# Rank of the score matmuls in a hand-made instruction order, and a scaling that two engines may take

## The chip, the cores and the metric

The kernel runs on one core of one Trainium2 chip. A core has five engines with a queue of instructions each: TensorE (PE, with its weight loads shown as PEld), VectorE (DVE), ScalarE (ACT), GpSimd (POOL) and SyncE (SP), which here issues most DMAs. Every engine works through its own queue in order and waits on semaphores for the others. The time is the device time of one execution in microseconds (us); where several runs are shown, their median.

## The reference, cut to what matters

Block-sparse attention (4 batches, 8 heads, 768 positions, 64 columns per head; blocks of 32) is followed by four causal attention "experts" on its output, of which each position uses the best two, weighted.

```python
mask = np.abs(blk_i - blk_j) <= 1
mask = mask | (blk_i == 0) | (blk_j == 0) | (blk_i == n_blocks - 1) | (blk_j == n_blocks - 1)
# and three sampled blocks of keys for every block of queries
attn = softmax(where(mask, scale * q @ k.T, -1e9));  x = attn @ v      # heads side by side: 512 columns
logits = x @ w_gate;  topk = best 2 of 4;  w = softmax over the two
for e in range(4):
    a = softmax(causal(scale * (x @ wq[e]) @ (x @ wk[e]).T))           # 768 x 768
    out += (w of e, 0 where not chosen) * (a @ (x @ wv[e]) @ wo[e])
```

## The kernel before, in words

**Units of work.** For each batch the sparse part works through six tiles of 128 queries, each in two halves of four heads: `tiles` (lines 645 to 724), called a U unit. Its scores (L671) put, for each block of 32 queries, the three neighbouring, three sampled and two end blocks of keys in a score tile `s`; one reduction on DVE (L676) takes the maxima, four exponents on ACT (L681) write the probabilities into a tile `p`, four transposes on PE in each of two steps (L687) and their copies (L383 on ACT or L387 on DVE) put them into `pt`, PV (L701) multiplies by the gathered values `va` and `vb`, DVE divides by the sums (L711 to L713), and two transposes (L718) with a split into a high and a low half (L399, L400) write x into `xh` and `xl`. The first and the last block of queries see all keys: `ends` (lines 576 to 643), two G units per batch, with scores L590 in two chunks of 512 and 256 keys, reductions L596, exponents L599, transposes L607, PV L616 and L626 to L635. They read their own scaled copy of the queries, `qz`.

The expert part projects x: `project_v` (L744), `project_qk` (L801, three products of high and low halves), and `gating`. `expert` (lines 808 to 891) handles one row of 128 positions of a pair of experts: scores L822 with the triangle added at L826, reductions L832, exponents L835 with their sums, a few small DVE operations for the denominators (L846 to L852), the scaling of the probabilities by 1/sum and gate weight (L859, on DVE), transposes L870, PV L887 and a split (L399, L400). Rows 4 and 5 have more than 512 keys: two score chunks, two `p` tiles, two `pt` tiles and four scalings; the other rows have one of each and two scalings. `project_o` (L901) multiplies by wo and stores.

**Loads.** Keys, queries and values come by DMA from SP. From batch 1 on the queries are scaled on POOL (L443, for `q` and `qz`), sampled keys are copied together on POOL (L501), values get a column of ones on POOL (L469), go to a scratch tensor in DRAM (L479) and are gathered from there for each tile of queries: neighbours and end blocks at L545 to L557 into `va` and `vb`, sampled blocks at L564, twelve DMAs for a tile.

**What sets the order.** Nothing is scheduled by a compiler. The program lists all units in a sequence (lines 932 to 939), where the projections of a batch are merged with the last sparse tiles of it and the first of the next batch, and the experts of a batch with the G units and the tiles 2 and 3 of the next. `Plan` (lines 66 to 193) then plays the list through with a cost for each operation: whenever an engine is free, it takes of the operations whose inputs are done the one with the lowest rank, `prio`, and issues it there and then. The rank of an operation is the place n of its unit in the sequence, (n, 0), unless it is given; ties go by the order in which operations were added. What `Plan` chooses is the fixed order in each engine's queue. An operation with several engines is offered to each of them, in the order ACT, DVE, PE, POOL, SP, and goes to the first that takes it. An operation is held back while its unit is more than `window` places ahead of the oldest unfinished unit, a DMA while its rank is more than `look` places ahead; and while the buffers it needs are all taken.

**Buffers.** Tiles come from rings (lines 231 to 257): two score tiles `s` and four tiles `w` in PSUM; four `p`, three `pt`, two `xn`, four `q`, two tiles of gathered keys, and one `va` and one `vb` for even and one for odd tiles of queries. A ring's slot is taken by the first operation that writes it and comes free with the last that reads it. A score operation takes its `s` tile and its `p` tiles at once; `pt` is taken by the first transpose and held until PV.

The functions that the change touches:

Of the kernel before, what the change touches and what calls it, by code (L numbers as in the profile page):

```python
# [14 lines left out]
ALU = mybir.AluOpType  # L15
# [3 lines left out]
SP = mybir.EngineType.SP  # L19
ACT = mybir.EngineType.Activation  # L20
DVE = mybir.EngineType.DVE
POOL = mybir.EngineType.Pool
# [174 lines left out]
def block_sparse_then_moe(ctx: ExitStack, tc: tile.TileContext, qT, kT, v, samp, wg, wq, wk, wv, wo, out):  # L197
    nc = tc.nc
# [10 lines left out]
    scale = 1.0 / float(D) ** 0.5  # L209
# [11 lines left out]
    def f(ap):  # L221
        return ap.bitcast(F32)

    pl = Plan(window=10, look=12, lat={"PE": 0.2, "ACT": 0.12, "DVE": 0.12, "POOL": 0.15, "SP": 0.1})

    def ring(name, n, shape, dt=F32, space=None, ordered=False):
        p = space or pool
# [210 lines left out]
    def scaled(b, n, q):  # L438

        if b == 0:  # L440
            copy(n, lambda: q.t, lambda: q.t, [(q, "raw")], [q], mul=scale)
        else:
            pl.add("POOL", 0.25 + 0.0012 * n, lambda: nc.gpsimd.tensor_scalar(q.t, q.t, scale, None, op0=ALU.mult),  # L443
                   r=[(q, "raw")], w=[q])

    def load_ends(b):
# [12 lines left out]
    def load_values(b):  # L459

        vn, d = rVN.get(), rScr.get()
        for t0 in range(0, NT, 2):
            ts = slice(t0, t0 + 2)
            if b:
                for t in (t0, t0 + 1):
                    x = rW.get()
                    dma(b, 0.5, lambda e, x=x, t=t: e.dma_start(x.t, v[b, 128 * t:128 * t + 128].rearrange("p h c -> p (h c)")),
                        w=[x], xfer=0.7)
                    pl.add("POOL", 0.9, lambda x=x, t=t: nc.gpsimd.tensor_copy(  # L469
                        vn.t[:, t, :, 0:D], x.t.rearrange("p (h c) -> p h c", h=H)), r=[x, "c_1"], w=[vn, (vn, t0)])  # L470
            else:
                x = rPT.get()
                y = lambda x=x: x.t.rearrange("p (t c) d -> p t (c d)", t=2)
                dma(b, 0.5, lambda e, y=y, t0=t0: e.dma_start(
                    y(), v[b, 128 * t0:128 * t0 + 256].rearrange("(t p) h c -> p t (h c)", p=128)), w=[x], xfer=1.4)
                for t in (t0, t0 + 1):
                    copy(512, lambda t=t: vn.t[:, t, :, 0:D], lambda y=y, i=t - t0: y()[:, i].rearrange("p (h c) -> p h c", h=H),
                         [x, "c_1"], [vn, (vn, t0)])
            dma(b, 0.6, lambda e, t0=t0, ts=ts: e.dma_start(  # L479
                d.t[128 * t0:128 * t0 + 256].rearrange("(t p) h c -> p t (h c)", p=128),  # L480
                vn.t[:, ts].rearrange("p t h c -> p t (h c)")), both=False, r=[(vn, t0), "zr"], w=[d], xfer=1.9)
        return vn, d
# [93 lines left out]
    def ends(b, pp_, st, X, unit):  # L576


        qz, k, vn = st["qz"], st["k"], st["vn"]
        ss, pps, pts = ([r.get() for _ in range(2)] for r in (rs, rP, rPT))  # L580
        sm, xb, o = rSm.get(), rW.get(), rw.get()
        pairs = (2 * pp_, 2 * pp_ + 1)
        chunks = ((0, 512), (512, 256))

        def sc(i, c0, cw):
            for j in range(2):
                for c, P4 in enumerate(pairs):
                    r = slice(64 * j, 64 * j + 64)
                    x = k.t + P4 * S + c0
                    nc.tensor.matmul(ss[i].t[64 * c:64 * c + 64, j, 0:cw], qz.t[r, P4], KK[r, x:x + cw],  # L590
                                     start=True, stop=True, tile_position=(64 * j, 64 * c), skip_group_check=True)

        for i, (c0, cw) in enumerate(chunks):
            pl.add("PE", 0.96 if cw == 512 else 0.5, lambda i=i, c0=c0, cw=cw: sc(i, c0, cw),
                   r=[qz] + [(k, P4) for P4 in pairs], w=[ss[i]] + [(x, "r") for x in pps], unit=unit)
            pl.add("DVE", 0.15 + 0.00208 * cw, lambda i=i, cw=cw: nc.vector.tensor_reduce(  # L596
                sm.t[:, 2 * i:2 * i + 2], ss[i].t[:, :, 0:cw], AX.X, op=ALU.max, negate=True), r=[ss[i]], w=[(sm, "m", i)], unit=unit)
            for j in range(2):
                pl.add("ACT", 0.27 + 0.00083 * cw, lambda i=i, j=j, c0=c0, cw=cw: nc.scalar.activation(  # L599
                    pps[j].t[:, c0:c0 + cw], ss[i].t[:, j, 0:cw], AF.Exp, bias=sm.t[:, 2 * i + j:2 * i + j + 1]),  # L600
                    r=[ss[i], (sm, "m", i)], w=[(pps[j], i)], unit=unit)
        chunk_factors(sm, unit)
        for j in range(2):
            for c0, n in ((0, 4), (4, 2)):
                w = rw.get()
                pl.add("PE", 0.09 + 0.11 * n, lambda j=j, c0=c0, n=n, w=w: [
                    nc.tensor.transpose(w.t[:, 128 * i:128 * i + 128], pps[j].t[:, 128 * (c0 + i):128 * (c0 + i) + 128], ident)  # L607
                    for i in range(n)], r=[(pps[j], 0 if c0 == 0 else 1), "c_a"], w=[w, (pts[j], "r")], unit=unit)
                evacuate(128 * n, lambda j=j, c0=c0, n=n: pts[j].t[:, c0:c0 + n].rearrange("p a b -> p (a b)"),
                         lambda w=w, n=n: w.t[:, 0:128 * n], [w], [pts[j]], unit=unit)  # L610

        def pv(j):
            for t in range(NT):
                x = (2 * (t // 4) + j) * VW
                for c, P4 in enumerate(pairs):
                    nc.tensor.matmul(o.t[64 * c:64 * c + 64, x:x + VW], pts[j].t[:, t, 64 * c:64 * c + 64],  # L616
                                     vn.t[:, t, 2 * P4 + j], start=t % 4 == 0, stop=t in (3, NT - 1), tile_position=(0, 64 * c),
                                     skip_group_check=True)

        for j in range(2):  # L620
            pl.add("PE", 0.85, lambda j=j: pv(j), r=pts + [vn], w=[o, (xb, "r")], unit=unit)

        def norm():
            ov = o.t[:, 0:4 * VW].rearrange("p (n c) -> p n c", c=VW)
            y = xb.t[:, 0:4 * VW].rearrange("p (n c) -> p n c", c=VW)
            nc.vector.tensor_tensor(y, ov, sm.t[:, 10:14, None].to_broadcast([128, 4, VW]), op=ALU.mult)  # L626
            nc.vector.tensor_tensor(y[:, 0:2], y[:, 0:2], y[:, 2:4], op=ALU.add)
            nc.vector.tensor_scalar(sm.t[:, 4:6], y[:, 0:2, D], EPS, None, op0=ALU.add)
            nc.vector.reciprocal(sm.t[:, 4:6], sm.t[:, 4:6])
            nc.vector.tensor_tensor(xb.t[:, 384:512].rearrange("p (j d) -> p j d", j=2), y[:, 0:2, 0:D],  # L630
                                    sm.t[:, 4:6, None].to_broadcast([128, 2, D]), op=ALU.mult)

        pl.add("DVE", 1.3, norm, r=[o, (sm, "e")], w=[xb, (sm, "n")], unit=unit)
        w = rw.get()
        pl.add("PE", 0.2, lambda: nc.tensor.transpose(w.t[:, 0:128], xb.t[:, 384:512], ident), r=[xb],  # L635
               w=[w, (X[0], "r"), (X[1], "r")], unit=unit)

        def at(x):
            x = x[:, pairs[0]]
            return sub_ap(x, 0, [x.ap[0], [S, 2], [S - 32, 2], [1, 32]])  # L640

        split(128, lambda: at(XH), lambda: at(XL), lambda: w.t[:, 0:128].rearrange("p (c a b) -> p c a b", c=2, a=2),
              [w], [(x, P4, "g") for x in X for P4 in pairs], unit)

    def tiles(b, t, pp_, st, X, unit):
# [3 lines left out]
        pairs = (2 * pp_, 2 * pp_ + 1)  # L649
# [22 lines left out]
                                         tile_position=(64 * j, 32 * g), skip_group_check=True)  # L672

        for i in range(2):
            pl.add("PE", 0.62, lambda i=i: sc(i), r=[q, (k, pairs[i]), kg], w=[s, (pp, "r")], unit=unit)
        pl.add("DVE", 1.22, lambda: nc.vector.tensor_reduce(sm.t[:, 0:4], s.t.rearrange("p j (t c) -> p (j t) c", t=2),  # L676
                                                            AX.X, op=ALU.max, negate=True), r=[s], w=[(sm, "m")], unit=unit)
        for i in range(2):
# [129 lines left out]
    def expert(b, st, p, r, unit):  # L808
# [19 lines left out]
        for i, (c0, cw) in enumerate(chunks):  # L828
            rd = [(qk, 0, 512 if r > 3 else 0), (qk, 1, 512 if c0 else 0), "c_b"]
            pl.add("PE", 0.08 + cw / 520 + (0.2 if c0 + cw == n else 0.0), lambda i=i, c0=c0, cw=cw: sc(i, c0, cw),  # L830
                   r=rd, w=[ss[i]] + [(x, "r") for x in pps], unit=unit)
            pl.add("DVE", 0.15 + 0.00208 * cw, lambda i=i, cw=cw: nc.vector.tensor_reduce(  # L832
                sm.t[:, 2 * i:2 * i + 2], ss[i].t[:, :, 0:cw], AX.X, op=ALU.max, negate=True), r=[ss[i]], w=[(sm, "m", i)], unit=unit)
            for j in range(2):
# [20 lines left out]
        for i, (c0, cw) in enumerate(chunks):  # L855
            for j in range(2):
                x = 10 + 2 * i + j
                f_ = lambda j=j, c0=c0, cw=cw: pps[j].t[:, p0[j] + c0:p0[j] + c0 + cw]
                pl.add("DVE", 0.13 + 0.00052 * cw, lambda f_=f_, x=x: nc.vector.tensor_scalar(  # L859
                    f_(), f_(), sm.t[:, x:x + 1], None, op0=ALU.mult),  # L860
                    r=[(pps[j], j, i), (sm, "d")], w=[(pps[j], j, "n", i)], unit=unit)
        pts = [rPT.get() for _ in range(2)] if two else [rPT.get()] * 2
        t0s = (0, 0) if two else (0, 4)
# [150 lines left out]
```

## Time and profile before

| | |
|---|---|
| median of 3 runs | 598.55 us (597.52 to 602.64) |
| the profiled execution | 603.58 us |
| its span, first to last instruction | 601.8 us |
| mean granted clock of PE | 0.963 |

The profile is that of one execution, and all numbers of stages and instructions below come from it. A busy share is the share of the span in which an engine had an instruction under way. A row of a group reads: line, engine, operation, what it writes <- what it reads, shapes, count | busy time in us, mean of one in ns | idle time of that engine just before, and what ended it. A row of waits reads: who waited <- for what: us in total, times, the longest. "PE w L607 <- ACT p L599" means that PE stood before the instruction of line 607 that writes `w`, until ACT's instruction of line 599 that writes `p` had ended. In a timeline row, start and duration in us stand in front and the idle time before it in brackets. The granted clock is TensorE's, as a share of full speed; it is either 1.00 or 0.50 at any moment, and a stretch's value is the mean.

| 40 equal slices of the span | |
|---|---|
| PE busy, tenths | 2787889967799999989799999998799999997896 |
| PE clock, tenths | 9899989978799999999799999999799999999999 |
| POOL busy, tenths | 2867604610002033413001211532101202000000 |

### The profile page before, as it was taken

How to read it: one execution, taken by the hardware profiler on the slowest of the kernel's cores; microseconds unless marked ns; L12 is line 12 of the kernel's file. 1: busy time of each engine (PE TensorE's matmuls, PEld its weight loads, DVE VectorE, ACT ScalarE, POOL GpSimd, SP SyncE). 2: the span in 40 equal slices, each digit the busy share in tenths (PEclk: the TensorE clock that was granted, in tenths of full speed). 3: DMA queues.
4: the chain of work that ended last, by engine and by line, in shares of the span. 5: the costliest groups of instructions: out<-in, count | busy, mean ns of one | idle time of the engine just before them, and what ended most of it. 6: DMA issues, size and time to landing. Idle time of an engine off the chain costs nothing.

```text
span 601.8 us, 23159 instructions
## 1 busy us (share of the span) xinstructions
PE 533.3 (89%) x9416; PEld 405.5 (67%) x9416; DVE 380.0 (63%) x1028; ACT 305.2 (51%) x844; POOL 138.8 (23%) x334
## 2 busy tenths in 40 slices
PE   2787889967799999989799999998799999997896
PEld 1576677854377688867556778886457678776674
DVE  4788644636687744446687873464787885356794
ACT  2576453535556654345474654353566564334654
POOL 2867604610002033413001211532101202000000
PEclk9899989978799999999799999999799999999999
DMA  7544467776110467775401274876601153000011
GB/s 254 175 105 122 95 173 244 207 184 168 43 38 20 119 196 221 209 173 137 108 2 53 62 205 117 290 169 169 153 2 36 37 145 103 21 2 1 2 36 71
DMA packets 58410, 70.25 MB, mean 117 GB/s; under 512 B 17792, under 2 KB 30208, under 8 KB 58304
## 3 DMA queue, kind: packets, MB, share of 16 engines
q1 hardware_dynamic: 53440, 65.88, 40.0%
q10 hardware_dynamic: 4864, 2.89, 1.6%
q8 instruction: 75, 1.23, 0.9%
q14 instruction: 31, 0.25, 0.2%
HBM read 55.92 MB, written 12.81 MB: 114 GB/s over the span
## 4 chain that ended last, share of the span: by engine, by line
PE 71%; DVE 14%; ACT 4%; issue 4%; DMA 2%; SPq 1%; POOL 0%; POOLq 0%; ACTq 0%; DVEq 0%
PE w L801 11%; PE s L671 9%; PE s L822 7%; PE w L701 7%; PE w L687 7%; PE w L887 7%; PE w L901 6%; PE w L744 5%; PE w L870 5%; DVE p L859 2%; DVE sm L832 2%; PE w L718 2%; ACT pt L383 2%; PE w L607 2%; PE w L616 1%
## 5 line engine op out<-in xcount | busy, mean ns | idle before, releaser
L383 ACT ACTIVATE pt<-w 128x512 f32<-128x512 f32 (+3 forms) x149 | 77.7, 543 | 70.6 <-PE w L870 28.8
L681 ACT ACTIVATE p<-s,sm 128x256 f32<-128x256 f32 x192 | 77.2, 478 | 46.2 <-DVE sm L676 46.0
L501 POOL COPY KK<-KK 128x128 f32 x213 | 54.2, 302 | 137.8 <-PE s L671 85.6
L835 ACT ACTIVATE p<-s,sm 128x512 f32<-128x512 f32 (+3 forms) x128 | 68.5, 545 | 18.5 <-DVE sm L832 13.8
L676 DVE TENSOR_REDUCE sm<-s 128x4 f32<-128x1024 f32 x48 | 58.5, 1221 | 27.1 <-PE s L671 26.8
L387 DVE COPY pt<-w 128x512 f32<-128x512 f32 (+3 forms) x91 | 52.6, 587 | 34.9 <-PE w L687 26.8
L443 POOL TENSOR_SCALAR q<-q 128x512 f32<-128x512 f32 x18 | 27.2, 1514 | 187.7 <-DMA q<-in_qT_dram 187.7
L832 DVE TENSOR_REDUCE sm<-s 128x2 f32<-128x1024 f32 (+3 forms) x64 | 54.3, 854 | 25.1 <-PE s L826 15.4
L671 PE MATMUL s<-KK,q 64*32 64x64 f32 (+1 forms) x3072 | 64.2, 278 | 3.8 <-ACT q L383 1.3
L671 PEld LDWEIGHTS s<-KK,q 64*32 64x32 f32 x3072 | 51.4, 107 | 17.3 <-issue 9.3
L687 PE MATMUL w<-ident,p 128*128 128x128 f32 x384 | 58.0, 282 | 2.9 <-ACT p L681 2.9
L822 PE MATMUL s<-qk 64*128 64x512 f32 (+3 forms) x256 | 58.8, 541 | 0.4 <-ACT p L681 0.3
L870 PE MATMUL w<-ident,p 128*128 128x128 f32 x336 | 50.5, 284 | 7.0 <-DVE p L859 5.4
L701 PE MATMUL w<-vb,pt 128*32 128x65 f32 x1536 | 50.5, 221 | 5.6 <-issue 5.6
L887 PE MATMUL w<-pt,vb 128*64 128x128 f32 x672 | 51.3, 282 | 3.4 <-DVE pt L387 1.9
L701 PE MATMUL w<-va,pt 128*32 128x65 f32 x1536 | 50.8, 224 | 3.5 <-issue 2.5
L887 PEld LDWEIGHTS w<-pt,vb 128*64 128x64 f32 x672 | 38.0, 138 | 19.9 <-DVE pt L387 5.3
L687 PEld LDWEIGHTS w<-ident,p 128*128 128x128 f32 x384 | 43.3, 143 | 10.4 <-ACT p L681 4.1
L870 PEld LDWEIGHTS w<-ident,p 128*128 128x128 f32 x336 | 37.5, 143 | 14.1 <-DVE p L859 3.4
L859 DVE TENSOR_SCALAR p<-p,sm 128x512 f32<-128x512 f32 (+3 forms) x128 | 46.0, 405 | 1.2
L701 PEld LDWEIGHTS w<-va,pt 128*32 128x32 f32 x1536 | 36.2, 109 | 15.2 <-issue 7.1
L801 PE MATMUL w<-xh,wqkh 128*128 128x512 f32 (+1 forms) x128 | 46.0, 359 | 0.0
(122 smaller groups left out, 951.0 us busy)
## 6 DMA issues: line engine op xcount, KB each, us to landing
vb<-scr SPq DMA_DIRECT2D x270, 65.0 KB, 2.7
va<-scr SPq DMA_DIRECT2D x12, 780.0 KB, 6.3
scr<-VN SPq DMA_DIRECT2D x12, 520.0 KB, 3.6
KK<-in_kT_dram SPq DMA_DIRECT2D x16, 384.0 KB, 5.6
out_dram<-ws SPq DMA_DIRECT2D x24, 256.0 KB, 2.2
ws<-in_v_dram SPq DMA_DIRECT2D x18, 256.0 KB, 4.1
q<-in_qT_dram SPq DMA_DIRECT2D x18, 256.0 KB, 4.2
va<-scr SPq DMA_DIRECT2D x6, 585.0 KB, 5.6
```

The costliest lines, as they stand in the source:

```text
L383: nc.scalar.activation(dst(), src(), AF.Copy, scale=1.0 if mul is None else mul)
L671: nc.tensor.matmul(dst, q.t[r, P4, 32 * g:32 * g + 32], src, start=True, stop=True, tile_position=(64 * j, 32 * g), skip_group_check=True)
L676: pl.add("DVE", 1.22, lambda: nc.vector.tensor_reduce(sm.t[:, 0:4], s.t.rearrange("p j (t c) -> p (j t) c", t=2), AX.X, op=ALU.max, negate ...
L681: pl.add("ACT", 0.47, lambda i=i, j=j, n=n: nc.scalar.activation(pp.t[:, 256 * n:256 * n + 256], s.t[:, j, 256 * i:256 * i + 256], AF.Exp, ...
L687: nc.tensor.transpose(w.t[:, 128 * c:128 * c + 128], pp.t[:, 512 * (c // 2) + 256 * i + 128 * (c % 2):][:, 0:128], ident)
L701: nc.tensor.matmul(o.t[32 * g:32 * g + 32, VW * n:VW * n + VW], pt.t[:, 4 * i + 2 * j + c, 32 * g:32 * g + 32], x.t[:, cl(g), h * VW:h * V ...
L801: nc.tensor.matmul(w.t[:, 0:cw], a[:, k, x], y[:, k, c0:c0 + cw], start=n == 0, stop=n == 3 * KT - 1)
L822: nc.tensor.matmul(ss[i].t[:, j, 0:cw], qk.t[x, 0, r * 128:(r + 1) * 128], qk.t[x, 1, c0:c0 + cw], start=True, stop=not last, tile_positio ...
L832: pl.add("DVE", 0.15 + 0.00208 * cw, lambda i=i, cw=cw: nc.vector.tensor_reduce(sm.t[:, 2 * i:2 * i + 2], ss[i].t[:, :, 0:cw], AX.X, op=AL ...
L835: pl.add("ACT", 0.47 + 0.00083 * cw, lambda i=i, j=j, c0=c0, cw=cw: nc.scalar.activation(pps[j].t[:, p0[j] + c0:p0[j] + c0 + cw], ss[i].t[ ...
L870: nc.tensor.transpose(w.t[:, 128 * i:128 * i + 128], pps[j].t[:, p0[j] + 128 * t:][:, 0:128], ident)
L887: nc.tensor.matmul(o.t[64 * j:64 * j + 64, 0:128], vb.t[:, t, e * D:(e + 1) * D], pts[j].t[:, t0s[j] + t], start=t == 0, stop=t == r, tile ...
```

## The change

- The score operations of the three kinds of units (L590, L671, L822 with L826) get the rank of the place six before their unit's, `(unit - AHEAD, 0)`. All else of a unit keeps its rank.
- `window` goes from 10 to 14, `look` from 12 to 16.
- The scaling of queries on POOL (L443) becomes a multiplication by the scale and a second one by 1.0 in one instruction.
- The scaling of experts' probabilities (L859) is offered to DVE and POOL; POOL's form multiplies by the factor of each row and by 1.0.
- `Plan`'s costs change for the scaling of queries (0.25 + 0.0012 n to 0.15 + 0.00095 n us), the copy of values on POOL (0.9 to 0.63) and DVE's scaling of probabilities (0.00052 to 0.00056 per column).

```diff
--- before.py
+++ after.py
@@ -221,7 +221,8 @@
     def f(ap):
         return ap.bitcast(F32)
 
-    pl = Plan(window=10, look=12, lat={"PE": 0.2, "ACT": 0.12, "DVE": 0.12, "POOL": 0.15, "SP": 0.1})
+    AHEAD = 6
+    pl = Plan(window=14, look=16, lat={"PE": 0.2, "ACT": 0.12, "DVE": 0.12, "POOL": 0.15, "SP": 0.1})
 
     def ring(name, n, shape, dt=F32, space=None, ordered=False):
         p = space or pool
@@ -440,7 +441,7 @@
         if b == 0:
             copy(n, lambda: q.t, lambda: q.t, [(q, "raw")], [q], mul=scale)
         else:
-            pl.add("POOL", 0.25 + 0.0012 * n, lambda: nc.gpsimd.tensor_scalar(q.t, q.t, scale, None, op0=ALU.mult),
+            pl.add("POOL", 0.15 + 0.00095 * n, lambda: nc.gpsimd.tensor_scalar(q.t, q.t, scale, 1.0, op0=ALU.mult, op1=ALU.mult),
                    r=[(q, "raw")], w=[q])
 
     def load_ends(b):
@@ -466,7 +467,7 @@
                     x = rW.get()
                     dma(b, 0.5, lambda e, x=x, t=t: e.dma_start(x.t, v[b, 128 * t:128 * t + 128].rearrange("p h c -> p (h c)")),
                         w=[x], xfer=0.7)
-                    pl.add("POOL", 0.9, lambda x=x, t=t: nc.gpsimd.tensor_copy(
+                    pl.add("POOL", 0.63, lambda x=x, t=t: nc.gpsimd.tensor_copy(
                         vn.t[:, t, :, 0:D], x.t.rearrange("p (h c) -> p h c", h=H)), r=[x, "c_1"], w=[vn, (vn, t0)])
             else:
                 x = rPT.get()
@@ -592,7 +593,8 @@
 
         for i, (c0, cw) in enumerate(chunks):
             pl.add("PE", 0.96 if cw == 512 else 0.5, lambda i=i, c0=c0, cw=cw: sc(i, c0, cw),
-                   r=[qz] + [(k, P4) for P4 in pairs], w=[ss[i]] + [(x, "r") for x in pps], unit=unit)
+                   r=[qz] + [(k, P4) for P4 in pairs], w=[ss[i]] + [(x, "r") for x in pps], unit=unit,
+                   prio=(unit - AHEAD, 0))
             pl.add("DVE", 0.15 + 0.00208 * cw, lambda i=i, cw=cw: nc.vector.tensor_reduce(
                 sm.t[:, 2 * i:2 * i + 2], ss[i].t[:, :, 0:cw], AX.X, op=ALU.max, negate=True), r=[ss[i]], w=[(sm, "m", i)], unit=unit)
             for j in range(2):
@@ -672,7 +674,7 @@
                                          tile_position=(64 * j, 32 * g), skip_group_check=True)
 
         for i in range(2):
-            pl.add("PE", 0.62, lambda i=i: sc(i), r=[q, (k, pairs[i]), kg], w=[s, (pp, "r")], unit=unit)
+            pl.add("PE", 0.62, lambda i=i: sc(i), r=[q, (k, pairs[i]), kg], w=[s, (pp, "r")], unit=unit, prio=(unit - AHEAD, 0))
         pl.add("DVE", 1.22, lambda: nc.vector.tensor_reduce(sm.t[:, 0:4], s.t.rearrange("p j (t c) -> p (j t) c", t=2),
                                                             AX.X, op=ALU.max, negate=True), r=[s], w=[(sm, "m")], unit=unit)
         for i in range(2):
@@ -828,7 +830,8 @@
         for i, (c0, cw) in enumerate(chunks):
             rd = [(qk, 0, 512 if r > 3 else 0), (qk, 1, 512 if c0 else 0), "c_b"]
             pl.add("PE", 0.08 + cw / 520 + (0.2 if c0 + cw == n else 0.0), lambda i=i, c0=c0, cw=cw: sc(i, c0, cw),
-                   r=rd, w=[ss[i]] + [(x, "r") for x in pps], unit=unit)
+                   r=rd, w=[ss[i]] + [(x, "r") for x in pps], unit=unit,
+                   prio=(unit - AHEAD, 0))
             pl.add("DVE", 0.15 + 0.00208 * cw, lambda i=i, cw=cw: nc.vector.tensor_reduce(
                 sm.t[:, 2 * i:2 * i + 2], ss[i].t[:, :, 0:cw], AX.X, op=ALU.max, negate=True), r=[ss[i]], w=[(sm, "m", i)], unit=unit)
             for j in range(2):
@@ -856,8 +859,9 @@
             for j in range(2):
                 x = 10 + 2 * i + j
                 f_ = lambda j=j, c0=c0, cw=cw: pps[j].t[:, p0[j] + c0:p0[j] + c0 + cw]
-                pl.add("DVE", 0.13 + 0.00052 * cw, lambda f_=f_, x=x: nc.vector.tensor_scalar(
-                    f_(), f_(), sm.t[:, x:x + 1], None, op0=ALU.mult),
+                pl.add(("DVE", "POOL"), (0.13 + 0.00056 * cw, 0.15 + 0.00095 * cw), (
+                    lambda f_=f_, x=x: nc.vector.tensor_scalar(f_(), f_(), sm.t[:, x:x + 1], None, op0=ALU.mult),
+                    lambda f_=f_, x=x: nc.gpsimd.tensor_scalar(f_(), f_(), sm.t[:, x:x + 1], 1.0, op0=ALU.mult, op1=ALU.mult)),
                     r=[(pps[j], j, i), (sm, "d")], w=[(pps[j], j, "n", i)], unit=unit)
         pts = [rPT.get() for _ in range(2)] if two else [rPT.get()] * 2
         t0s = (0, 0) if two else (0, 4)
```

## The prediction

> **What bounds the kernel now.** I read the page first (engine totals), then the stretches by stage with the granted clock, then the waits inside those stages.
>
> ```profile
> span 601.8 us, 23159 instructions
> PE 533.3 (89%) x9416; PEld 405.5 (67%) x9416; DVE 380.0 (63%) x1028; ACT 305.2 (51%) x844; POOL 138.8 (23%) x334
> ```
>
> TensorE (PE) sets the time; nothing in this change takes a matmul away. A gain can only come from PE's idle time, 601.8 - 533.3 = 68.5 us, and from time in which PE runs at half clock. So I looked for both by stage. The rows of the stage view give PE, PEld, DVE, ACT and POOL busy time, then the granted clock, the DMA share and GB/s.
>
> ```profile
> 136.00:160.00 24.00, 17.59 (x285) 10.95 (x281) 17.37 (x54) 13.39 (x37) 1.49 (x1) 0.91 0.52 127
> 281.00:306.30 25.30, 20.93 (x250) 12.87 (x250) 18.98 (x56) 13.98 (x42) 2.80 (x7) 0.87 0.33 78
> 425.50:446.50 21.00, 16.23 (x160) 10.18 (x156) 15.18 (x45) 10.66 (x30) 1.62 (x1) 0.84 0.38 92
> 48.00:77.00 29.00, 21.64 (x594) 17.22 (x582) 20.26 (x48) 16.35 (x42) 18.83 (x33) 1.00 0.47 110
> 549.00:568.20 19.20, 14.18 (x121) 9.73 (x119) 14.27 (x46) 12.07 (x40) 0.00 (x0) 0.91 0.01 1
> ```
>
> The first three are the heads of the expert phases of batches 0, 1 and 2: PE idles 24.0 - 17.59 = 6.4, 4.4 and 4.8 us, together 15.6. The fourth is the stage with the weights (7.4 idle), the fifth the head of the last batch's experts (5.0). The clock by stretch shows where it is halved:
>
> ```profile
> 145.60:149.00 3.40, 3.40 (x17) 1.63 (x17) 1.78 (x3) 1.19 (x4) 1.30 (x1) 0.50 0.96 263
> 159.30:166.10 6.80, 5.86 (x18) 2.01 (x20) 2.38 (x6) 2.77 (x8) 0.00 (x0) 0.50 0.00 0
> 289.00:295.80 6.80, 5.33 (x46) 3.17 (x48) 2.88 (x7) 2.26 (x7) 0.00 (x0) 0.50 0.61 147
> 428.90:435.80 6.90, 4.91 (x38) 2.75 (x40) 3.40 (x7) 1.84 (x5) 0.69 (x1) 0.51 0.70 160
> 77.40:80.80 3.40, 3.40 (x23) 3.17 (x30) 0.96 (x2) 1.76 (x4) 0.00 (x0) 0.50 0.37 81
> 555.20:558.60 3.40, 3.02 (x14) 2.69 (x16) 2.76 (x9) 1.64 (x5) 0.00 (x0) 0.50 0.00 0
> 128.60:135.40 6.80, 5.26 (x39) 3.55 (x38) 2.52 (x6) 1.05 (x3) 0.00 (x0) 0.50 0.59 154
> 268.50:271.90 3.40, 3.40 (x16) 3.16 (x16) 1.12 (x4) 0.56 (x2) 0.43 (x1) 0.50 0.74 196
> ```
>
> Each lies in or just behind a stage with stalls. PE work at half clock costs about half its duration: in the four stretches of the expert heads (3.40 + 5.86 + 5.33 + 4.91) / 2 = 9.75 us. What PE waited for, one view for each of the stages (expert heads in order, weights, last batch):
>
> ```profile
> PE w L607 <- ACT p L599: 2.2, 1, 2.2
> PE s L590 <- ACT p L835: 1.5, 2, 1.2
> ...
> PE w L607 <- ACT p L599: 3.0, 2, 2.6
> ...
> PE w L607 <- ACT p L599: 3.7, 2, 3.3
> ...
> PE w L718 <- DVE xn L713: 3.0, 2, 1.8
> PE w L687 <- ACT p L681: 2.9, 3, 1.9
> ...
> PE w L870 <- DVE p L859: 4.1, 3, 2.3
> ```
>
> At the expert heads PE mostly waits at the transposes of an "ends" unit (L607), because its scores (L590) were issued just before and reduction, exponent and transposes follow one another. Its inputs had been there long: for batch 1 the scaled qz is ready at 218.6 us, and the wait at L607 ends at 290.47.
>
> ```profile
> 217.79 0.85 POOL L443 TENSOR_SCALAR qz<-qz 128x256 f32<-128x256 f32 x1 [0.25 <-DMA qz<-in_qT_dram]
> 290.47 0.69 PE L607 MATMUL w<-ident,p 128*128 128x128 f32 x2 [2.62 <-ACT p L599]
> ```
>
> **The change part by part.**
>
> *Scores six places ahead (expert heads).* No instruction is added; scores at L590, L671 and L822 take a lower rank, so PE issues them as soon as a score tile (ring s, 2) and a probability tile (ring p, 4) are free, during the projections at L801, which is work for PE alone. Reductions and exponents then run under cover, and the projections held back fill what was idle. Of the 15.6 us, 2.2 + 1.5 + 3.0 + 3.7 = 10.4 (two thirds) end at an ends unit, which can be brought forward; the rest hangs on experts whose q and k come from the projection itself. Reachable: 15.6 + 9.75 = 25.3 us. Bounds 0 and -25.3; I take 60%, a little under the two thirds since two score tiles limit the lead: **-15.2**.
>
> *Weights stage.* Reachable 7.4 + 3.40 / 2 = 9.1. DVE and POOL are at 20.26 and 18.83 of 29 there, so scores alone feed engines that are already loaded. Bounds 0 and -9.1; I take a third: **-3.0**.
>
> *Last batch.* Reachable 5.0 + 3.02 / 2 = 6.5. No other unit covers the experts here, and most of it ends with the scaling at L859, which the next unit's early scores can cover in part. Bounds 0 and -6.5; about half: **-3.0**.
>
> *POOL shares L859.* Prices: DVE's rows (last batch) and POOL's for 128x512, and what happened where both ran at once.
>
> ```profile
> L859 DVE TENSOR_SCALAR p<-p,sm 128x512 f32<-128x512 f32 x12 | 5.3, 483 | 0.2
> L859 DVE TENSOR_SCALAR p<-p,sm 128x256 f32<-128x256 f32 x8 | 2.4, 348 | 0.0
> L469 POOL COPY VN<-ws 128x512 f32<-128x512 f32 x18 | 10.8, 618 | 2.0 <-DMA ws<-in_v_dram 1.8
> L443 POOL TENSOR_SCALAR q<-q 128x512 f32<-128x512 f32 x18 | 27.2, 1514 | 187.7 <-DMA q<-in_qT_dram 187.7
> 427.98 1.62 POOL L443 TENSOR_SCALAR q<-q 128x512 f32<-128x512 f32 x1 [5.89 <-DMA q<-in_qT_dram]
> 428.04 1.70 DVE L859 TENSOR_SCALAR p<-p,sm 128x512 f32<-128x512 f32 x3
> ```
>
> The three DVE scalings beside POOL's instruction took 1.70 us instead of 0.48 + 0.35 + 0.35 = 1.18: such pairs get in each other's way. The two-multiplication form has no row. Bounds: 0.62 (a copy of that size) and 2 x 1.51 = 3.03 (two passes of today's form). The new plan says 0.64 for it; where its other new figures have a row (the copy of v 0.63 against 0.618, DVE's scaling 0.42 against 0.483) they fit within 15%, so I go by the low end, though the nearest row by operation is 1.51. A two-chunk expert has four scalings, now 2 x 0.48 + 2 x 0.35 = 1.66 us in a row. If POOL takes one of each size at 0.62 and about 0.45 and the engines overlap fully, 1.07; if they take turns, 0.48 + 0.62 + 0.35 + 0.45 = 1.90. At 1.51 and about 0.85 in turns: 3.19. In three batches PE has other units, so the price is nothing while that cover lasts; without it, each unit would add its difference to PE's wait. In the last batch (4 two-chunk units, 8 others with half as much work, so 8 in effect) it is 8 x -0.6 = -5, 8 x +0.24 = +2 or 8 x +1.5 = +12. I take turns in part: **+1.0**.
> The Trainium skill, "SBUF — State Buffer", section "Who interferes with whom", says that DVE in a two-port mode and GpSimd share a port pair that one holds for its whole instruction; the 1.70 against 1.18 agrees. By that rule the term is +2 and not +1, the result 585.0.
>
> *Loads and gathers.* A score issues no DMA, but frees its q and gathered-key tiles earlier, so POOL's copies (L501) and q's loads start earlier, loads also by look 12 to 16, on the same SP queue as the gathers of v. Gathers already end four stalls of PE (the views of 100 to 135, 255 to 270 and 400 to 412 us; "issue" here is a wait for a landing that the view doesn't name):
>
> ```profile
> PE w L701 <- issue: 5.0, 2, 4.7
> PE s L671 <- POOL q L443: 1.1, 1, 1.1
> PE s L671 <- POOL KK L501: 0.2, 1, 0.2
> ...
> PE w L801 <- issue: 1.8, 1, 1.8
> PE s L671 <- issue: 0.9, 1, 0.9
> ...
> PE w L701 <- issue: 2.3, 1, 2.3
> ...
> 271.69 8.80 SPq L564 DMA_DIRECT2D vb<-scr  x12
> vb<-scr SPq DMA_DIRECT2D x270, 65.0 KB, 2.7
> ```
>
> That is 10.0 us, and (5.26 + 3.40) / 2 = 4.3 at half clock. One tile's gather is 8.80 us of issue and 2.7 to landing, and it starts when the tile two before has left va/vb through PV, which earlier scores push back. PE also gets there sooner. Bounds -10 (stalls gone) and +12 (one gather, 11.5, once more); I take **+3.0**.
>
> *q scaled on POOL in the other form; new costs.* 18 instructions at 0.62 to 3.03 instead of 1.51. POOL is busy 23%, and PE waited for this line once (1.1 us, the row above), so the work of other tiles hides it; bounds -1, and +5 where a longer one blocks DVE as at 428 us. I take **0**. The lower planned costs of copying v change only order.
>
> *Older work behind a score.* PE works in order: if a score's input is late on the chip, the older transposes and PV behind it wait, and ACT and DVE for their results. Scores' waits on POOL came to 1.3 us before (q 1.1, KK 0.2). Bounds 0 and +10; I take **+2.6**, twice those.
>
> Sum: -15.2 - 3.0 - 3.0 + 1.0 + 0 + 3.0 + 2.6 = -14.6. The profiled execution took 603.6 us (span 601.8, 1.8 around it), which makes 589.0; it lies 5.0 above the median of the runs, 598.55, so I forecast **584.0** (-2.4%).
> The Trainium skill, "TensorE: Matmul & The Clock Gate", Part 1, has the clock halved after an idle window of about 3.4 us. Here it is 0.50 at 289.0 though the longest stall of that stage is 2.6, so the trace decides; by the page the 9.75 would not go with these stalls, and the result would be 0.6 x 9.75 = 5.9 later, 589.9.
>
> **The rivals.**
> 1. *All chain stalls go:* -25.3 - 9.1 - 6.5 + 3.0 = -37.9, so 560.6. For it: inputs lie ready 70 us. Against: two score tiles, and expert heads need the projection.
> 2. *Gathers take the gain:* PE arrives about 6 us earlier per batch at a gather that SP issues no sooner, three times: -21.2 + 18 = -3, 595.5. For it: the 4.7 us wait. Against: PE hides gathers elsewhere (only 10 us of waits in all).
> 3. *Slower: tiles take the three pt slots.* Younger tiles, now through their exponent early, get transposed in a gap and hold pt until PV, which needs their gather of v (11.5 us); an expert or ends unit needs two slots and stands still. Three stages at 11.5, half covered, are +17; with half of the 15.2 kept, +9.5: 608. It decides from the second such stage on. For it: pt has 3 slots and L701 already waits for gathers. Against: older transposes still rank first.
> 4. *POOL's form stays at 1.51:* +12 in place of +1: 595.
> 5. *The lead does not come about:* rings s and p are full, a quarter of 21.2 remains and the give-back of 3.0: -2.3, 596.
>
> **How the numbers follow.** Forecast 0.47 (its own range 574 to 592), rivals in order 0.12, 0.13, 0.16, 0.05, 0.07. A measurement of this kernel can tell about 1% (592.6 and 604.5) from no change. Faster: forecast and rival 1, 0.59, and a little of the others, 0.60; same: rivals 2, 4 and 5, 0.24; slower: rival 3, 0.16. The range 562 to 608 leaves out about half of rival 1 and half of rival 3, near 0.14.
>
> **What would show it.** Right: no wait at L607 for L599 over 1 us in the expert heads; PE idle there under 8 us in sum; clock 0.95 or more in those stages; POOL's new scalings of 128x512 near 0.64 us; about half of L859's instructions on POOL, and DVE's 128x512 ones above 483 ns where POOL runs beside them. Wrong: waits L701 <- issue that grow past 10 us (rival 2), waits of L870 or L607 behind tiles' PV (rival 3), POOL's form at 1.5 us or more (rival 4), or L590 again within 5 us of its L607 (rival 5).

## The result and the profile after

The changed kernel takes 565.6 us (median of 4 runs, 564.6 to 569.6) against 600.6 us for the kernel before beside it: a ratio of 0.943, 95% interval 0.936 to 0.951, so 5.7% faster. The forecast was 584.0 us, 2.4% faster; the measured time is 18 us below it, outside the forecast's own range of 574 to 592 and near the rival that had all chain stalls go (560.6). Runs more than 1.5% above the fastest of their kernel (three of b_window's ten, one of the kernel before) are left out of the medians and ratios below.

The page after, its span and its totals of the engines:

```profile
span 564.8 us, 23268 instructions
PE 511.7 (91%) x9416; PEld 398.2 (71%) x9416; DVE 373.4 (66%) x972; ACT 286.6 (51%) x813; POOL 173.1 (31%) x421
```

Of the 37.0 us between the two spans, PE's idle time gave 68.5 - 53.1 = 15.4 and its busy time 21.6. PE work at half clock fell from 38.0 to 13.4 us (all half-clock stretches of the two profiles, the short ones at the start included), at half its duration 12.3; the other 9.3 us of busy time I can't put down to one cause. The profiled execution of before was 5 us above the 598.55 us of the first table and had more half-clock time than the same kernel in a hardly different order (b_jit below: 21.1 us of PE work), so part of the 12.3 belongs to that execution.

Where the expert phases begin (from the last projection of q and k of a batch to its first output projection), first the three stages of before, then those of after; columns as in the stage view of the prediction:

```profile
121.30:173.60 52.30, 40.84 (x621) 25.91 (x619) 31.20 (x87) 24.63 (x66) 4.47 (x13) 0.84 0.47 113
276.30:314.00 37.70, 33.19 (x455) 20.84 (x453) 28.70 (x75) 21.82 (x60) 4.46 (x13) 0.91 0.27 65
416.00:454.30 38.30, 33.25 (x457) 20.90 (x454) 29.41 (x75) 21.91 (x60) 5.78 (x14) 0.91 0.32 78
```

```profile
123.10:161.60 38.50, 33.55 (x573) 23.08 (x572) 29.43 (x77) 20.41 (x63) 7.15 (x11) 1.00 0.65 153
262.90:290.50 27.60, 25.64 (x344) 17.10 (x342) 23.66 (x63) 18.11 (x52) 6.62 (x11) 1.00 0.32 79
397.70:425.30 27.60, 25.65 (x344) 17.10 (x343) 24.04 (x63) 18.09 (x52) 6.62 (x11) 1.00 0.32 77
```

PE's idle time there falls from 11.5 + 4.5 + 5.0 = 21.0 us to 4.9 + 2.0 + 2.0 = 8.9, and the clock is 1.00 throughout. The stages are also shorter because work left them (344 matmuls instead of 455 in the second). Of these 111, 64 are the scores of a tile (L671) and 8 those of experts, which now run earlier; the rest is a different mix of other units' work.

What PE waited for after, the whole run, longest first:

```profile
PE w L703 <- issue: 9.1, 6, 3.0
PE s L591 <- DVE qz L390: 7.8, 1, 7.8
PE w L609 <- ACT p L601: 6.5, 5, 3.4
PE w L637 <- DVE ws L632: 5.6, 3, 3.5
PE s L673 <- issue: 5.0, 7, 1.4
PE w L703 <- DMA vb<-scr: 4.7, 6, 1.2
...
PE w L874 <- POOL p L864: 2.2, 5, 0.6
```

The lines have moved by two to four: L609 is the old L607, L703 the old L701, L874 the old L870. The wait at the ends units' transposes was 12.1 us in the run before, of which 3.2 belong to the start; it is 6.5, of which 3.4 belong to the start:

```profile
PE w L607 <- ACT p L599: 12.1, 6, 3.3
```

The waits at PV that end with a gather or with a release that the view doesn't name ("issue"), and the "issue" waits at the tiles' scores, have grown to 9.1 + 4.7 + 5.0 = 18.8 us; before they were 8.1 + 0.9 = 9.0. That the 5.0 at the scores (L673) hang on gathers of values isn't shown: scores read none, and and one of the waits ends together with POOL's copy of gathered keys (at 38.48 us).

The groups by shape: POOL's share of the scaling, what is left on DVE, and the scaling of queries in the new form.

```profile
L864 POOL TENSOR_SCALAR p<-p,sm 128x512 f32<-128x512 f32 x36 | 27.4, 770 | 164.6 <-DVE sm L853 69.3 <-DVE sm L855 65.2 <-ACT qk L384 13.3
L444 POOL TENSOR_SCALAR q<-q 128x512 f32<-128x512 f32 x18 | 11.1, 620 | 4.7 <-DMA q<-in_qT_dram 4.6
L863 DVE TENSOR_SCALAR p<-p,sm 128x128 f32<-128x128 f32 x16 | 6.8, 428 | 0.2
L863 DVE TENSOR_SCALAR p<-p,sm 128x512 f32<-128x512 f32 x12 | 6.1, 504 | 0.8
```

Two multiplications in one take 620 ns where one took 1514. POOL does 87 of the 128 scalings (its row on the page follows below) and DVE 41. Where both run they hold each other up. POOL's 770 ns compare with 697 for the same size in a_pool below, where DVE does none of these scalings; the 620 of the row L444 are for a constant factor instead of one for each row. DVE's 428 for 128x128 compare with the last batch of before, where POOL did nothing:

```profile
L859 DVE TENSOR_SCALAR p<-p,sm 128x128 f32<-128x128 f32 x8 | 1.9, 281 | 0.0
```

The copies out of PSUM, on the pages of before (first) and after:

```profile
L383 ACT ACTIVATE pt<-w 128x512 f32<-128x512 f32 (+3 forms) x149 | 77.7, 543 | 70.6 <-PE w L870 28.8
L387 DVE COPY pt<-w 128x512 f32<-128x512 f32 (+3 forms) x91 | 52.6, 587 | 34.9 <-PE w L687 26.8
L859 DVE TENSOR_SCALAR p<-p,sm 128x512 f32<-128x512 f32 (+3 forms) x128 | 46.0, 405 | 1.2
```

```profile
L864 POOL TENSOR_SCALAR p<-p,sm 128x512 f32<-128x512 f32 (+3 forms) x87 | 52.6, 615 | 214.4 <-DVE sm L853 94.7
L388 DVE COPY pt<-w 128x512 f32<-128x512 f32 (+3 forms) x118 | 70.4, 613 | 29.0 <-PE w L689 22.4
L384 ACT ACTIVATE pt<-w 128x512 f32<-128x512 f32 (+3 forms) x122 | 62.7, 529 | 37.1 <-PE w L689 20.3
```

DVE lost 27 us of scaling (46.0 less 6.8 + 6.1 and two smaller shapes, 19.0) and took 17.8 us more of these copies, which left ACT (77.7 to 62.7): most of what POOL took over was passed on through DVE to ACT, so that ACT was relieved too.

### The profile page after: what moved, and what is told of

Same layout as the page of the kernel before. It is cut to its first block, busy times and chain, and to the rows that moved or that the text cites. A ratio compares the mean times of both kernels' runs of the same rounds, so it can differ in the third digit from the quotient of the medians.

```text
span 564.8 us, 23268 instructions
## 1 busy us (share of the span) xinstructions
PE 511.7 (91%) x9416; PEld 398.2 (71%) x9416; DVE 373.4 (66%) x972; ACT 286.6 (51%) x813; POOL 173.1 (31%) x421
## 4 chain that ended last, share of the span: by engine, by line
PE 74%; DVE 9%; issue 5%; DMA 3%; SPq 3%; ACT 1%; POOL 1%; POOLq 0%; DVEq 0%; ACTq 0%
PE w L803 10%; PE s L673 10%; PE w L703 8%; PE w L689 7%; PE s L824 7%; PE w L746 6%; PE w L905 6%; PE w L874 6%; PE w L891 5%; DVE sm L835 2%; DMA vb<-scr 2%; PE w L720 2%; PE w L618 2%; SPq L565 2%; PE s L828 1%
## 5 line engine op out<-in xcount | busy, mean ns | idle before, releaser
L864 POOL TENSOR_SCALAR p<-p,sm 128x512 f32<-128x512 f32 (+3 forms) x87 | 52.6, 615 | 214.4 <-DVE sm L853 94.7
L683 ACT ACTIVATE p<-s,sm 128x256 f32<-128x256 f32 x192 | 77.7, 478 | 41.3 <-DVE sm L678 30.3
L388 DVE COPY pt<-w 128x512 f32<-128x512 f32 (+3 forms) x118 | 70.4, 613 | 29.0 <-PE w L689 22.4
L384 ACT ACTIVATE pt<-w 128x512 f32<-128x512 f32 (+3 forms) x122 | 62.7, 529 | 37.1 <-PE w L689 20.3
L838 ACT ACTIVATE p<-s,sm 128x512 f32<-128x512 f32 (+3 forms) x128 | 68.3, 541 | 24.9 <-DVE sm L835 19.1
L673 PE MATMUL s<-KK,q 64*32 64x192 f32 (+1 forms) x3072 | 66.4, 283 | 6.4 <-issue 5.0
L673 PEld LDWEIGHTS s<-KK,q 64*32 64x32 f32 x3072 | 52.6, 109 | 20.3 <-issue 13.8
L703 PE MATMUL w<-vb,pt 128*32 128x65 f32 x1536 | 51.4, 220 | 10.8 <-issue 6.0
L689 PE MATMUL w<-ident,p 128*128 128x128 f32 x384 | 54.9, 277 | 1.1 <-ACT p L683 1.1
L874 PE MATMUL w<-ident,p 128*128 128x128 f32 x336 | 50.3, 282 | 5.5 <-POOL p L864 2.2
L703 PE MATMUL w<-va,pt 128*32 128x65 f32 x1536 | 50.5, 223 | 3.1 <-issue 3.0
L824 PE MATMUL s<-qk 64*128 64x512 f32 (+3 forms) x256 | 51.4, 488 | 0.0
L703 PEld LDWEIGHTS w<-vb,pt 128*32 128x32 f32 x1536 | 40.5, 109 | 10.6 <-issue 8.4
L891 PE MATMUL w<-pt,vb 128*64 128x128 f32 x672 | 45.9, 279 | 0.6 <-DVE pt L388 0.5
L874 PEld LDWEIGHTS w<-ident,p 128*128 128x128 f32 x336 | 37.0, 142 | 12.4 <-issue 3.9
L703 PEld LDWEIGHTS w<-va,pt 128*32 128x32 f32 x1536 | 36.8, 109 | 11.8 <-issue 8.1
L803 PE MATMUL w<-xh,wqkl 128*128 128x512 f32 (+1 forms) x128 | 43.4, 339 | 1.0 <-issue 1.0
```

Of the source, the lines that this page charges most:

```text
L384: nc.scalar.activation(dst(), src(), AF.Copy, scale=1.0 if mul is None else mul)
L388: nc.vector.tensor_copy(dst(), src())
L673: nc.tensor.matmul(dst, q.t[r, P4, 32 * g:32 * g + 32], src, start=True, stop=True, tile_position=(64 * j, 32 * g), skip_group_check=True)
L683: pl.add("ACT", 0.47, lambda i=i, j=j, n=n: nc.scalar.activation(pp.t[:, 256 * n:256 * n + 256], s.t[:, j, 256 * i:256 * i + 256], AF.Exp, ...
L689: nc.tensor.transpose(w.t[:, 128 * c:128 * c + 128], pp.t[:, 512 * (c // 2) + 256 * i + 128 * (c % 2):][:, 0:128], ident)
L703: nc.tensor.matmul(o.t[32 * g:32 * g + 32, VW * n:VW * n + VW], pt.t[:, 4 * i + 2 * j + c, 32 * g:32 * g + 32], x.t[:, cl(g), h * VW:h * V ...
```

## The experiments

Theory 1 at first: the early scores carry the gain. Theory 2: POOL's share carries it. Theory 3: window and look do. Ratios are to the kernel before on the same chip, with 95% intervals.

**One part undone, one part alone.**

a_lead0:

```diff
-    AHEAD = 6
+    AHEAD = 0
```

> The changed kernel with the lead of the scores set to 0; window 14, look 16, POOL's share and the other form stay. Theory 1 (the early scores carry the gain, by keeping PE above half busy in every stretch of 3.4 us, so that the clock isn't halved): 585 to 598 us, at least five stretches at half clock after the first 40 us. Theory 2 (POOL's share carries it, by relieving DVE in the expert stages): 565 to 572 us. Theory 3 (window and look carry it): 565 to 572 us as well.

583.8 us, ratio 0.976 (0.972 to 0.980). The time is just below theory 1's 585 to 598, and the clock isn't as it had it: after the first 40 us the profile has two stretches at half clock (at 149.0 and 258.2 us), not five or more.

a_dve:

```diff
-                pl.add(("DVE", "POOL"), (0.13 + 0.00056 * cw, 0.15 + 0.00095 * cw), (
-                    lambda f_=f_, x=x: nc.vector.tensor_scalar(f_(), f_(), sm.t[:, x:x + 1], None, op0=ALU.mult),
...
+                pl.add("DVE", 0.13 + 0.00056 * cw, lambda f_=f_, x=x: nc.vector.tensor_scalar(
+                    f_(), f_(), sm.t[:, x:x + 1], None, op0=ALU.mult),
```

> The changed kernel with the scaling of the experts' probabilities on DVE alone, at the new planned cost. Theory 1: 565 to 574 us. Theory 2: 585 us or more. Theory 3: 565 to 574 us.

587.0 us, 0.978 (0.973 to 0.984).

b_lead6 (the kernel before; the same `prio` at the three kinds of scores):

```diff
+    AHEAD = 6
...
-                   r=[qz] + [(k, P4) for P4 in pairs], w=[ss[i]] + [(x, "r") for x in pps], unit=unit)
+                   r=[qz] + [(k, P4) for P4 in pairs], w=[ss[i]] + [(x, "r") for x in pps], unit=unit,
+                   prio=(unit - AHEAD, 0))
```

> The kernel before with nothing but the scores' rank six places ahead (window 10, look 12, scaling on DVE, old costs, old form of scaling queries). Theory 1: 568 to 582 us. Theory 2 and theory 3: 594 to 604 us.

584.4 us, 0.977 (0.973 to 0.980).

b_share (the kernel before, L859 offered to both engines as in the change):

```diff
-                pl.add("DVE", 0.13 + 0.00052 * cw, lambda f_=f_, x=x: nc.vector.tensor_scalar(
...
+                pl.add(("DVE", "POOL"), (0.13 + 0.00056 * cw, 0.15 + 0.00095 * cw), (
```

> The kernel before with nothing but the scaling of experts' probabilities offered to POOL. Theory 1: 592 to 602 us, the half-clock stretches at the expert heads still there. Theory 2: 570 to 580 us. Theory 3: 594 to 604 us.

586.6 us, 0.979 (0.975 to 0.983). Of the half-clock stretches at the expert heads, two are left in the first batch (133.2 and 160.5 us) and none in the next two.

No theory holds. Theory 1 expected almost nothing of the share, and it brings 11.6 us alone; theory 2 expected almost nothing of the lead, and it brings 13.8 alone. Undoing either in the changed kernel loses 18 to 21 us. What PE waits for in b_lead6 says what the lead doesn't reach:

```profile
PE w L703 <- issue: 9.5, 7, 4.4
PE w L637 <- DVE ws L632: 8.6, 7, 3.2
PE w L873 <- DVE p L862: 7.9, 6, 1.7
...
PE w L609 <- ACT p L601: 6.3, 3, 3.4
PE w L720 <- DVE xn L715: 5.9, 5, 2.2
```

The old wait at the ends units is 6.3, about as in the changed kernel, but PE waits 8.6 + 7.9 + 5.9 us for DVE: its scaling (L862) and divisions (L632, L715). In the changed kernel these are 5.6, 0.9 (POOL's scalings 2.2) and 0.2.

Where PE idles says more. In the body of the first batch's expert phase, from its first output projection to its last, the rows of before, b_lead6 and the changed kernel are:

```profile
173.60:221.70 48.10, 46.59 (x758) 34.68 (x760) 35.26 (x105) 28.31 (x87) 9.28 (x24) 1.00 0.35 101
154.50:209.80 55.30, 50.65 (x827) 37.77 (x829) 41.20 (x121) 33.89 (x104) 9.22 (x24) 1.00 0.31 90
161.60:202.80 41.20, 40.60 (x745) 30.89 (x743) 30.77 (x90) 25.27 (x78) 13.16 (x36) 1.00 0.43 123
```

In the heads of three batches the lead alone takes PE's idle time from 21.0 us to 7.8, but in their bodies it raises it from 3.7 to 14.8. Over the whole span PE idles 67.0 us in b_lead6, against 68.5 before and 67.1 in b_jit: the lead alone moves stalls and hardly removes any. Its gain is in PE's busy time (513.3 us against 533.3 and 525.4), in which the work at half clock is 9.6 us against 38.0 and 21.1. That made theory 1a: the lead takes the waits for late exponents at the heads, the share those for a late DVE behind them.

**The two together, and what POOL's part rests on.**

b_both is b_lead6 and b_share in one (both diffs above).

> The kernel before with the lead of six and POOL's share, and nothing else of the change (window 10, look 12, old form and costs of scaling queries). Alone the two gave 584.4 and 586.6 us. Theory 1a (they complete each other: the lead empties the expert heads and moves the stall into the bodies, to DVE's scaling; POOL's share takes that away): 562 to 573 us. Theory 4 (the first 14 us are all that either can give, the rest comes from window, look or costs): 580 to 586 us.

572.7 us, 0.957 (0.951 to 0.964). 598.4 less 13.8 and 11.6 would be 573: in time the two add up, and neither needs the other. The bodies of the three expert phases, where PE idled 14.8 us in b_lead6, are down to 0.7 + 0.2 + 0.6 = 1.5. Not all waits for DVE are gone: the scaling's is 0.4 now, but the tiles' divisions (L715) keep theirs, and POOL's scalings add some.

```profile
PE w L720 <- DVE xn L715: 6.0, 6, 2.1
PE w L874 <- POOL p L864: 5.3, 6, 2.9
```

All of PE's waits that DVE ended, without the one at the start, were 22.4 us before, 24.9 in b_lead6 and 13.5 here, with 5.3 for POOL's scalings.

a_form1, the same instructions in the same places but for POOL's form:

```diff
-                    lambda f_=f_, x=x: nc.gpsimd.tensor_scalar(f_(), f_(), sm.t[:, x:x + 1], 1.0, op0=ALU.mult, op1=ALU.mult)),
+                    lambda f_=f_, x=x: nc.gpsimd.tensor_scalar(f_(), f_(), sm.t[:, x:x + 1], None, op0=ALU.mult)),
```

> The changed kernel, in the same order of instructions, with POOL's scaling of probabilities as one multiplication instead of two in one. 87 instructions at up to 1.5 us instead of 0.6. Theory 1a, with POOL's scaling on the path of the experts: 580 to 600 us, waits of PE for POOL's scaling over 15 us. Theory 5 (POOL has room, its form matters little): 565 to 572 us.

580.0 us, 0.970 (0.964 to 0.977), at the low edge of what 1a gave; the waits reach 13.1 us and not 15:

```profile
L864 POOL TENSOR_SCALAR p<-p,sm 128x512 f32<-128x512 f32 x36 | 58.8, 1640 | 148.5 <-DVE sm L853 66.2 <-DVE sm L855 53.3 <-ACT qk L384 13.6
```

```profile
PE w L874 <- POOL p L864: 13.1, 15, 1.8
```

So the second multiplication, which computes nothing, is worth 14 us here: it is what lets POOL do a 128x512 scaling in 0.70 to 0.77 us instead of 1.64.

a_pool:

```diff
-                pl.add(("DVE", "POOL"), (0.13 + 0.00056 * cw, 0.15 + 0.00095 * cw), (
-                    lambda f_=f_, x=x: nc.vector.tensor_scalar(f_(), f_(), sm.t[:, x:x + 1], None, op0=ALU.mult),
+                pl.add("POOL", 0.15 + 0.00095 * cw, (
```

> The changed kernel with the scaling of probabilities on POOL alone. Theory 1b (relief of DVE is what counts): 562 to 570 us. Theory 1c (two engines side by side, so that the four scalings of an expert end sooner, is what counts): 574 to 590 us, PE's waits for POOL's scaling well over the 2.2 us of the changed kernel.

565.6 us, 0.944 (0.937 to 0.952), the same as the change. The groups by shape:

```profile
L863 POOL TENSOR_SCALAR p<-p,sm 128x512 f32<-128x512 f32 x48 | 32.8, 697 | 161.9 <-DVE sm L853 66.3 <-DVE sm L855 60.7 <-DVE o L401 15.8
L863 POOL TENSOR_SCALAR p<-p,sm 128x256 f32<-128x256 f32 x32 | 15.1, 485 | 10.1 <-DVE sm L853 10.1
```

```profile
PE w L873 <- POOL p L863: 3.1, 6, 1.3
```

A two-chunk expert's four scalings now take 2 x 0.70 + 2 x 0.49 = 2.4 us in a row, longer than the 1.66 on DVE before, and nothing is lost. What counts is that DVE is rid of them, not that two engines finish them sooner (theory 1b; 1c falls). Whether DVE's own relief pays, or that of ACT by the copies that DVE then takes, no run separates.

b_window (window 14, look 16 in the kernel before):

```diff
-    pl = Plan(window=10, look=12, lat={"PE": 0.2, "ACT": 0.12, "DVE": 0.12, "POOL": 0.15, "SP": 0.1})
+    pl = Plan(window=14, look=16, lat={"PE": 0.2, "ACT": 0.12, "DVE": 0.12, "POOL": 0.15, "SP": 0.1})
```

> The kernel before with window 14 and look 16 and nothing else. Theory 1a: 590 to 604 us. Theory 3 (window and look carry the gain): 570 to 585 us.

604.5 us, 1.009 (1.004 to 1.014), a little beyond the upper edge: alone these cost about 1%. Theory 3 falls.

**The last 7 us, and chance.** From 572.7 to 565.6 there are window and look, the form of scaling queries, and costs.

a_window10 (the line above turned round, in the changed kernel):

> The changed kernel with window 10 and look 12 as before, all else of the change in it. Lead and share without the rest gave 572.7 us, all of it 565.6. If window and look, with the lead, carry the last 7 us: 571 to 576 us. If the form and costs of scaling queries and copying values carry them: 563 to 568 us.

568.6 us, 0.951 (0.947 to 0.955); between the two expectations.

a_form1q:

```diff
-            pl.add("POOL", 0.15 + 0.00095 * n, lambda: nc.gpsimd.tensor_scalar(q.t, q.t, scale, 1.0, op0=ALU.mult, op1=ALU.mult),
+            pl.add("POOL", 0.15 + 0.00095 * n, lambda: nc.gpsimd.tensor_scalar(q.t, q.t, scale, None, op0=ALU.mult),
```

> The changed kernel, in the same order of instructions, with the scaling of queries as one multiplication (1.5 us instead of 0.6 for each of 18). As the prediction had it (POOL's free time hides it): 563 to 569 us. If a longer hold on DVE or a later q costs: 570 to 578 us.

566.5 us, 0.947 (0.939 to 0.954): no difference, as the prediction had it.

a_jit and b_jit (in each kernel one latency of the plan, which deals the order anew):

```diff
-lat={"PE": 0.2, "ACT": 0.12, "DVE": 0.12, "POOL": 0.15, "SP": 0.1})
+lat={"PE": 0.21, "ACT": 0.12, "DVE": 0.12, "POOL": 0.15, "SP": 0.1})
```

> The changed kernel, planned with a latency of 0.21 us instead of 0.20 behind PE, which should bring nothing by itself and only deals the order anew. If differences of some us between orders are chance: anywhere from 558 to 575 us. If the order's quality comes from the rules: 563 to 569 us.

568.4 us, 0.949 (0.944 to 0.953).

> The kernel before, planned with a latency of 0.21 us instead of 0.20 behind PE. If differences of some us between orders are chance: anywhere from 588 to 608 us. If the order's quality comes from the rules: 595 to 602 us. In either case the lead and the share keep most of their 26 us if theory 1a holds.

598.3 us, 1.002 (0.999 to 1.005). These two deals moved the time by 3 us at most, so the order's quality comes from the rules, as far as two deals can say. So a_window10's 3 us are no more than such a deal, and how the last 7 us divide among window, look and costs stays open.

**The clock, and the size of the lead.** The clock's changes lie on a grid of 3.41 us. In the profile before, all nine stretches of the grid with PE busy for under half of it (0.08 to 0.48) at full clock were followed by half clock, and none of the 147 with 0.51 or more was. In the other profiles a few between 0.41 and 0.58 went the other way.

b_warm keeps PE busy through one stall of the old order:

```diff
                 pl.add("PE", 0.09 + 0.11 * n, lambda j=j, c0=c0, n=n, w=w: [
+                    nc.tensor.transpose(w.t[:, 0:128], ident, ident) for _ in range(16 if (j, c0) == (0, 4) else 0)] + [
                     nc.tensor.transpose(w.t[:, 128 * i:128 * i + 128], pps[j].t[:, 128 * (c0 + i):128 * (c0 + i) + 128], ident)
```

> The kernel before in its old order; ahead of one transpose step of each ends unit (the one that PE waits for at the expert heads) PE transposes the identity 16 times into the tile that the step then overwrites, 1.7 us of extra PE work for each of 8 units, 13.6 us in all. Theory 1d (PE below half busy in a stretch of 3.4 us halves the clock in the next): the half-clock stretches behind the expert heads of batches 1 and 2 (289.0 and 428.9 us in the kernel before) are gone, and the extra work costs far less than its 13.6 us: 590 to 603 us. If the clock does not hang on that: the half-clock stretches stay, and 603 to 613 us.

605.1 us, 1.013 (1.005 to 1.021): a loss, 2 us beyond what theory 1d gave and inside the range of its rival. It is 5.9 us over the kernel before beside it, for extra transposes that take 17.0 us of PE's time in this trace. The stages of the expert heads in its profile:

```profile
136.00:160.00 24.00, 20.19 (x321) 13.75 (x316) 16.90 (x49) 13.15 (x37) 1.49 (x1) 1.00 0.67 165
281.00:310.00 29.00, 25.98 (x306) 17.48 (x307) 23.64 (x64) 16.86 (x49) 2.45 (x5) 1.00 0.32 80
425.00:452.00 27.00, 25.18 (x252) 17.46 (x251) 20.80 (x57) 15.57 (x44) 1.60 (x1) 1.00 0.29 71
```

The clock is 1.00 in all three, 0.91, 0.87 and 0.84 before, so the stretches are gone where they were to go. The test is weaker than it looks. In the first two stages PE is busy for 0.75 and 0.67 of a stretch of the grid with the extra transposes and would be for 0.24 and 0.16 without them; in the third it would be over 0.5 even without. The half-clock stretches that stood at 128.6 and 268.5 us are gone too, where nothing was added, and one stretch with 0.47 kept the full clock. The profiled execution is also the fastest of the four: its granted clock is 0.988, the others have 0.971 to 0.977, and the kernel before beside it has 0.963 to 0.980.

a_lead3 and a_lead12 (`AHEAD = 3`, `AHEAD = 12`):

> The changed kernel with a lead of three places. If scores only have to pass the projection in front of them: 563 to 572 us. If the lead has to cover a whole unit's chain: 573 to 582 us, between lead 0 (583.8) and lead 6 (565.6).

579.6 us, 0.970 (0.962 to 0.978).

> The changed kernel with a lead of twelve places, window 14 as it is. If the rings (two score tiles, four probability tiles) cap the lead: 563 to 570 us. If a longer lead displaces older work: 572 to 585 us.

565.3 us, 0.943 (0.937 to 0.950). Three places bring 4 us of the 18, six all, and twelve no more. No run is clearly faster than the changed kernel.

## Why the prediction was right and wrong

- *The lead (terms for expert heads, weights, last batch, loads and older work: -15.2 - 3.0 - 3.0 + 3.0 + 2.6 = -15.6).* The size is right, in part by luck: alone it measured -13.8 (b_lead6). The stall at L607 went as argued and the heads' idle time fell by 13 us, but most of it came back in the bodies, which I had no term for, so that the total fell by 1.5 us at most. The gain shows as shorter busy time of PE, less half clock among it. In the changed kernel the waits that I reckoned to gathers rose by 9.8 us (18.8 against 9.0), where the +3.0 allowed less.
- *POOL shares L859 (+1.0).* This is the step that failed: alone it measured -11.6 (b_share), and undoing it in the changed kernel costs 21 (a_dve). I priced the four scalings of one expert in a row and said that other units cover them in three batches, "the price is nothing while that cover lasts". That reckons only whether the row gets longer, and puts what DVE gains by losing the work at nothing. a_pool shows the mistake: a longer row on another engine costs nothing, and with all 128 scalings off DVE the gain stays whole. My bounds (-5 to +12) came from the row alone and did not hold the result. How the relief reaches PE is shown in part: PE's idle time in the bodies of b_lead6, 14.8 us, is 1.5 in b_both. Part of that is other units' work that stands behind the scalings: from 303.98 to 310.57 us of b_lead6 DVE does scalings, reductions and copies of several units without a gap. But at the longest waits for the scaling in these bodies (1.6 to 1.7 us, at 168.5, 302.8 and 443.1 us) DVE had idled 0.6 to 0.9 us just before the expert's reduction, so there the wait is the expert's own chain and not a queue. How the 11.6 us divide stays open.
- *What is missing in the sum.* Of the 20 us between -14.6 and the measured -35, 12.6 are this term. About 7 (572.7 to 565.6) came with window, look and costs, for which I had no gain; how they divide is open, as said above.
- *POOL's form.* The choice of 0.62 over 1.51 was right (620 ns in the row L444), and it mattered more than I said: 14 us (a_form1), where rival 4 had 11.
- *Scaling of queries: 0.* Right (a_form1q).
- *The clock.* I let it go in proportion to the stalls, at 60%. By the grid it is a step: a stretch either falls under about half busy or it doesn't, and in the heads of the profile after none does. The Trainium skill's rule ("TensorE: Matmul & The Clock Gate", Part 1), an idle window of about 3.4 us, doesn't fit here either, if idle means without work: in the heads the clock fell behind stretches in which PE was busy for 0.41 to 0.48. How much half clock an execution has is in part chance: the kernel before has granted clocks of 0.960 to 0.982 over its executions, in one and the same order.
- *The rivals.* The first came nearest (560.6), though not for its reason: the chain stalls did not all go. The second was half right, since the waits above grew by 9.8 us, but they didn't take the gain. No sign of the third: a lead of twelve, which would bring it on more, costs nothing. The fifth falls with b_lead6.
- *The port pair.* Both engines do hold each other up, as the Trainium skill ("SBUF — State Buffer", section "Who interferes with whom") has it: 770 against 697 ns on POOL, with and without DVE's scalings beside it. That costs little here: with all scalings on POOL the time is the same (a_pool). To let this price stand for the whole effect of the share was the mistake.
- *The signs.* The clock is 1.00 in the heads, as named. Three signs of being right did not come: a wait at L609 of 1.7 us is left in the first head, POOL's 128x512 scalings take 770 ns and not 640, and POOL does 87 of the 128 and not half. Of the signs of being wrong, the waits for gathers at PV came nearest to their limit of 10 us: 9.1 by the name that I gave, 13.8 with the landings that the view names.

## What to carry to other kernels

Price an instruction that leaves an engine by all that this engine does in the stage in question, not only by the chain it belongs to, and look at the busy share by stage: DVE has 63% over the span before, but 73 to 76% in the expert phases' bodies and 84% in the heads of b_lead6's second and third batch. A share alone decides nothing either: in the changed kernel DVE has 86 to 87% in these heads, and PE idles 2.0 us in each. In a kernel bound by PE, rank what feeds the other engines ahead of what only PE needs, and look for the stall that comes next: here it stood at DVE once the lead had moved the first, and the two changes added up. When a plan's order is dealt anew, deal it once more with a change that means nothing, to see how much is chance (3 us here).

## What the runs showed of the hardware that I had not expected

- On POOL, scaling 128x512 by a constant takes 620 ns with two multiplications in one instruction and 1514 with one; by a factor for each row it takes 697 to 770 (a_pool, after) and 1640 (a_form1).
- The clock's halving follows PE's busy share on a grid of 3.41 us, with the limit near one half, so one stall of 1.8 us can be followed by 3.4 us at half clock (before, at 265.1 us).
